# k weights of block 0 loaded ahead of two x tiles of block 1, and k of two token tiles computed between their q and the q of the next two

## The chip, the cores and the metric

The kernel runs on one core of a Trainium2 chip. A core has five engines that run at the same time, each through its own list of instructions: TensorE (PE; its weight loads are listed apart as PEld), VectorE (DVE), ScalarE (ACT), GpSimd (POOL) and SyncE (SP), which here only issues DMA transfers. The metric is the device time of one execution in microseconds (us). Before the change it is 202.04, the median of three runs (201.27 to 202.22).

## The reference

```python
xn = _layernorm(x)                       # x: 1 x 2048 x 512, bf16
# A: 32 heads of 16; W = 8 keys at distances 0, 2, .. 14
q, k, v = split(xn @ wqkv)
logits = einsum('bhsd,bhswd->bhsw', q, kg) * scale      # kg: k gathered at pos - 2*w
attn = _softmax(where(mask, logits, -1e9))
a = einsum('bhsw,bhswd->bhsd', attn, vg).reshape(B, S, D) @ wo
# B: gated MLP, F = 1376, Fh = 688
z = gelu(xn @ w_in)
z1, z2 = z[..., :Fh], _layernorm(z[..., Fh:])
g = einsum('ts,bsf->btf', w_sp, z2) + b_sp[None, :, None]   # w_sp: 2048 x 2048
return x + a + einsum('bsf,fd->bsd', z1 * g, w_out)
```

## The kernel before

**Tiling.** The 2048 tokens are 16 tiles of 128. Tile (j, tb) holds the tokens from 512·tb + 128·j on; the four tiles with the same j make a block, and the work goes block by block, j = 0 to 3. x lies in `r_x` (seen through `xall`), is normalised there in place, and is transposed into `xnT`, so that the 512 features lie along the partitions in four chunks (kc). All projections read `xnT`.

**A tile's way into `xnT`.** DVE measures a tile (`bn_stats`, L213 or L217) and aggregates (`bn_aggr`, L220). The inverse root comes from ACT (`ln_root`, L223), or for block 3 from POOL (`ln_root_pool`), an addition (L226) and a power (L227) on 128x1. DVE scales the tile (`ln_apply`, L231). The tiles of block 0 and the first two of block 1 are transposed by PE into PSUM (L238, L248) and copied to `xnT` by ACT or DVE (L242, L252, L253); the others are transposed by a DMA on SP's queue (`tr_dma`, L257).

**q and k.** The q and k weights lie in `r_w` (seen through `wqk`) in four quarters each, one per kc, 128 KB. One projection of a block, `qk_part(pq, j, m, ...)` (L321), fills half of q (m = 0, 1) or half of k (m = 2, 3) in PSUM; ACT casts it into `r_qk` (L337). For block 0, q is computed tile by tile (`q_tile`, L327) as the tiles come, and k afterwards for all four tiles at once.

**Products and logits.** For half a block of queries (a group g; there are eight) DVE multiplies q with four shifted views of k in four instructions, one per chunk c (`prod_c`, L361, 128x2048, 1.22 us each). Two additions per group (`pair_add` L370, `pair_add2` L373) fold the four chunks into one, and PE sums over the 16 dimensions of a head with a matmul against `rsel` (`logits`, L381). Then come softmax, the weighted sum of v (L445, L449 on DVE), and the output projection.

**The gated MLP.** w_in's second half gives z2 (L263 on PE, gelu on ACT at L281, squares at L287), its first half z1 (L263, L312). g is w_sp·z2 (L470), 448 matmuls, with w_sp transposed by DMA.

**PSUM** is shared by two pools: `ps_mm` has three buffers of 128x1024 f32, `ps_aux` two of 128x512 f32. An instruction that wants a new tile waits until a buffer's last reader is done.

**Order.** The program is scheduled by hand: each engine runs its instructions in the order in which the program issues them. The start (loads, layernorm, q and k of blocks 0 and 1) is written out as calls. All that follows is a string, `ORDER`, of tokens that stand for steps, a name and its numbers:

```python
z1.3   z2 matmuls of tile (1,3)      zg1.3  its gelu         zs1.3  its squares
q2.3   qk projection m=3, block 2    qc2.3  its cast         p1.2   product of group 1, chunk 2
a1 b1  the two additions of group 1  L1     its logits       Lc1    their cast
X0 Xg0 z1 matmuls and gelu           G0 U0  g matmuls, gate  w3     a DMA transpose of w_sp
```

Of the kernel before, what the change touches and what calls it, by code (L numbers as in the profile page):

```python
# [7 lines left out]
BF16 = mybir.dt.bfloat16  # L8
F32 = mybir.dt.float32
# [30 lines left out]
CHUNKS = (1, 1, 1, 1, 1, 1, 1, 1)  # L40
ORDER = """
z1.3 z2.0 z1.2 z2.2 zg1.3 p0.1 zg2.0 zg1.2 q2.2 zg2.2 p0.3 zs2.2 q2.3 p1.2 qc2.2 p1.3 q2.1 qc2.3 p1.0
z1.0 p0.2 qc2.1 w3 z2.1 p0.0 zg1.0 zs1.0 q2.0 p2.2 zg2.1 a1 z2.3 qc2.0 w2 zg2.3 p2.3 halo zs2.0 z3.0 p2.0 z1.1
w0 zg3.0 b1 z0.1 zg1.1 p2.1 zs2.3 X0 a0 zg0.1 z3.2 Xg0 zs1.1 z3.3 a2 zg3.2 z3.1 zs1.2 zg3.3 z0.2 b0 zg3.1 X4
b2 zg0.2 zs3.3 L0 L1 Xg4 q3.1 p3.2 zs3.1 p3.0 Lc0 q3.0 Lc1 p3.1 qc3.1 q3.2 p3.3 qc3.0 zs0.1 a3 z0.3 qc3.2 q3.3
zg0.3 p4.1 zs1.3 p4.0 z0.0 qc3.3 X1 p4.2 zg0.0 zs0.3 X2 p4.3 Xg1 X5 st.0 zs2.1 st.1 a4 Xg2 L2 V6 zs0.2 zs3.2
b3 Xg5 V2 b4 Vc6 zs0.0 p5.3 L3 V5 zs3.0 p5.2 Vc2 V1 st.2 p5.1 Vc5 p5.0 V0 st.3 a5 w4 Lc2 Vc1 V4 st.4 Vc0 w1
N1.1 V3 N2.0 Vc4 N1.0 b5 Lc3 V7 N0.0 Vc3 M0.0 N1.2 M0.1 L5 N0.2 L4 Vc7 N3.3 X6 N0.1 M0.2 N0.3 late X3 N3.1
N1.3 N2.1 G0.0 N2.2 Xg6 N2.3 N3.2 N3.0 G0.1 p7.1 G0.2 M0.3 G0.3 p7.2 G4 p6.0 Gi0 w6 Lc4 p6.3 Xg3 p6.2 E0 p7.3
G3 p6.1 U0 S0.0 p7.0 a6 w9 G1 Gi3 Gi4 S0.1 b6 a7 G2 Gi1 w7 U1 S0.2 b7 S0.3 w5 S0.4 Lc5 R0 L6 L7 G6 Lc6 A0 Gi2  # L50
Lc7 U2 U4 mask T4 U3 M1.0 A1 T2 G7 A2 Gi6 w8 A3 wo1.2 A4 T0 A5 X7 M1.1 Gi7 A6 wo1.3 xr0 G5 A7 Xg7 A8 w10 M1.2
A9 w12 U7 A10 X8 Gi5 A11 X10 T1 A12 G8 Xg10 A13 Xg8 wo1.0 A14 T7 M1.3 A15 G9 Gi8 A16 A17 E1 A18 A19 wo0.2
wo0.3 G10 wo0.1 U6 wo1.1 U5 Gi9 wo0.0 A20 T3 S1.0 S1.1 A21 X9 S1.2 G12 A22 S1.3 Gi10 T5 A23 S1.4 T6 A24 Xg9
w15 A25 X15 A26 Gi12 w14 X12 R1 Xg15 X11 A27 Xg12 w11 A28 O0 Xg11 A29 A30 A31 Or0 O1 A32 A33 A34 Or1 U8 Oh0.0
A35 A36 Oh0.1 Fe0.0 A37 Fe0.1 A38 G14 Fe0.2 Fe0.3 F0.2 F0.0 F0.1 s0.0 A39 s0.1 F0.3 A40 xr1 A41 Oh1.0 w13 A42
U10 Oh1.1 Fe1.0 U9 T8 Gi14 A43 Fe1.1 A44 T10 X13 A45 G11 s0.2 T9 A46 s0.3 F1.0 A47 A48 G13 F1.1 Gi11 s1.1 Xg13
U11 U12 Fe1.2 A49 T12 A50 A51 X14 A52 G15 Xg14 Fe1.3 U14 Gi13 F1.3 F1.2 A53 s1.2 T11 A54 T14 A55 O2 Gi15 s1.0
A56 U15 U13 T15 A57 Or2 xr2 Oh2.0 A58 A59 s1.3 Oh2.1 T13 Fe2.0 Fe2.1 xr3 F2.0 O3 Fe2.2 Fe2.3 F2.2 F2.1 s2.0
s2.2 F2.3 s2.1 s2.3 Or3 Of Oh3.1 end
# [10 lines left out]
def kernel(  # L70
# [98 lines left out]
    def load_wqk(E, s):  # L169
        for kc in range(C):  # L170
            E.dma_start(wqk[:, s, kc], A_wqkv[kc * P:(kc + 1) * P, s * D:(s + 1) * D])

    def load_x(E, j, b0, b1):
        for tb in range(b0, b1):
            E.dma_start(xall[:, j, tb], xblk[j][:, tb])
# [4 lines left out]
    load_x(A, 0, 2, 4)  # L180
    load_wqk(SP, 0)
    load_x(SP, 1, 0, 2)
    load_wqk(SP, 1)
    load_x(SP, 1, 2, 4)
    load_x(SP, 2, 0, 4)
    for kc in range(C):
        SP.dma_start(w_z2[:, kc], B_w_in[kc * P:(kc + 1) * P, FH:F])
# [21 lines left out]
    def ln_stats(i, parts=1):  # L209
        j, tb = i % 4, i // 4  # L210
        w = D // parts
        for h in range(parts):
            V.bn_stats(stats[:, i, 6 * h:6 * h + 6], xall[:, j, tb, w * h:w * h + w])  # L213
        ln_agg(i, parts)

    def ln_bn(i):
        V.bn_stats(stats[:, i, 0:6], xall[:, i % 4, i // 4, :])  # L217

    def ln_agg(i, parts=1):
        V.bn_aggr(mv[:, i, :], stats[:, i, 0:6 * parts])  # L220

    def ln_root(sl):
        A.activation(rstd[:, sl], mv[:, sl, 1], ACT.Abs_reciprocal_sqrt, bias=eps_t[:])  # L223

    def ln_root_pool(i):
        G.tensor_tensor(rstd[:, i:i + 1], mv[:, i, 1:2], eps_t[:], ALU.add)  # L226
        G.tensor_tensor(rstd[:, i:i + 1], rstd[:, i:i + 1], mhalf[:], ALU.pow)  # L227

    def ln_apply(i):
        j, tb = i % 4, i // 4  # L230
        V.tensor_scalar(xall[:, j, tb, :], xall[:, j, tb, :], mv[:, i, 0:1], rstd[:, i:i + 1],  # L231
                        ALU.subtract, ALU.mult)

    def tr(i):
        j, tb = i % 4, i // 4
        pt = ps_aux.tile([P, C, P], BF16, name="pt", tag="aux")
        for c in range(C):
            PE.transpose(pt[:, c, :], xall[:, j, tb, c * P:(c + 1) * P], ident[:])  # L238
        return pt

    def tr_copy(i, pt, c0=0, c1=C):
        A.copy(xnT[:, c0:c1, i * P:(i + 1) * P], pt[:, c0:c1, :])  # L242

    def tr2(i):
        j, tb = i % 4, i // 4
        pts = [ps_aux.tile([P, 2, P], BF16, name="pt", tag="aux") for _ in range(2)]
        for c in range(C):
            PE.transpose(pts[c // 2][:, c % 2, :], xall[:, j, tb, c * P:(c + 1) * P], ident[:])  # L248
        return pts

    def tr_copy2(i, pts):
        A.copy(xnT[:, 0:2, i * P:(i + 1) * P], pts[0][:])  # L252
        V.tensor_copy(xnT[:, 2:4, i * P:(i + 1) * P], pts[1][:])  # L253

    def tr_dma(i):
        j, tb = i % 4, i // 4
        SP.dma_start_transpose(xnT[:, :, i * P:(i + 1) * P], xall[:, j, tb, :])  # L257
# [66 lines left out]
    def q_tile(tb, kcs):  # L324
        for kc in kcs:
            for c in range(C):
                PE.matmul(pqs[c // 2][:, c % 2, tb * P:(tb + 1) * P], wqk[:, 0, kc, c:D:C],  # L327
                          xnT[:, kc, 4 * tb * P:(4 * tb + 1) * P], start=(kc == 0 and tb % 2 == 0), stop=(kc == C - 1 and tb % 2 == 1))
# [252 lines left out]
    def blk(j):  # L581
        return [4 * tb + j for tb in range(TB)]

    def col(i):
        return slice(i, i + 1)

    def blk_cols(j):
        return slice(j, NT, 4)

# [4 lines left out]

    t0, i1 = blk(0), blk(1)
    i2, i3 = blk(2), blk(3)
    warm_up(10)
    for n in range(2):
        ln_stats(t0[n], 2)
        ln_root(col(t0[n]))  # L600
    for n in range(2):
        ln_apply(t0[n])
    pts = [tr(t0[n]) for n in range(2)]
    tr_copy(t0[0], pts[0], 0, 2)
    tr_copy(t0[0], pts[0], 2, 4)
    tr_copy(t0[1], pts[1], 0, 2)
    warm_up(2, 1)
    pqs = [qk_tile() for _ in range(3)]
    ln_stats(t0[2])
    ln_root(col(t0[2]))  # L610
    tr_copy(t0[1], pts[1], 2, 4)
    q_tile(0, (0, 1))
    q_tile(0, (2,))
    q_tile(1, (0, 1))
    q_tile(0, (3,))
    ln_bn(t0[3])
    ln_apply(t0[2])
    ln_agg(t0[3])
    pt2 = tr2(t0[2])
    q_tile(1, (2, 3))  # L620
    ln_root(col(t0[3]))
    tr_copy2(t0[2], pt2)
    ln_apply(t0[3])
    q_tile(2, (0, 1))
    pt3 = tr2(t0[3])
    q_tile(2, (2, 3))
    tr_copy2(t0[3], pt3)
    q_tile(3, (0, 1))
    q_tile(3, (2, 3))
    ln_stats(i1[0])  # L630
    ln_root(col(i1[0]))
    qk_copy(pqs[0], 0, 0)
    ln_stats(i1[1])
    ln_root(col(i1[1]))
    qk_part(pqs[2], 0, 2, 0, 4, (0,))
    ln_apply(i1[0])
    qk_part(pqs[2], 0, 2, 0, 4, (1,), kcs=range(2))
    pt = tr(i1[0])
    qk_part(pqs[2], 0, 2, 0, 4, (1,), kcs=range(2, 4))
    ln_stats(i1[2])  # L640
    qk_copy(pqs[1], 0, 1)
    ln_root(col(i1[2]))
    ln_apply(i1[1])
    tr_copy(i1[0], pt)
    ln_bn(i1[3])
    ln_apply(i1[2])
    tr_dma(i1[2])
    ln_agg(i1[3])
    pq3 = qk_tile()
    qk_part(pq3, 0, 3, 0, 4, (0,), kcs=range(2))  # L650
    pt = tr(i1[1])
    qk_part(pq3, 0, 3, 0, 4, (0,), kcs=range(2, 4))
    tr_copy(i1[1], pt)
    ln_root(col(i1[3]))
    ln_apply(i1[3])
    tr_dma(i1[3])
    load_x(SP, 3, 0, 4)
    qk_part(pq3, 0, 3, 0, 4, (1,))
    qk_copy(pqs[2], 0, 2)
    qk_copy(pq3, 0, 3)  # L660
    for n in range(4):
        ln_stats(i2[n])
    ln_root(slice(2, 7, 4))
    ln_root(slice(10, 15, 4))
    A.preload_act_table_set("gelu_apprx_tanh_and_others")
    table[0] = "gelu"
    for i in i2:
        ln_apply(i)
        tr_dma(i)
    for n in range(3):  # L670
        ln_stats(i3[n])
        ln_root_pool(i3[n])
    ln_apply(i3[0])
    tr_dma(i3[0])
    ln_stats(i3[3])
    ln_root_pool(i3[3])
    for i in i3[1:3]:
        ln_apply(i)
        tr_dma(i)
    pqs = [qk_tile() for _ in range(3)]  # L680
    for c in range(3):
        qk_part(pqs[c], 1, c, 0, 2)
    pa3 = ps_aux.tile([P, 2, 2 * P], F32, name="pa3", tag="aux")
# [73 lines left out]
```

## Time and profile before

The profile is one execution. "Span" reaches from its first instruction to its last; the three timed runs are beside it. Busy time is the sum of an engine's instructions and overlaps among engines.

| | us |
|---|---|
| span of the profiled execution | 199.9 |
| timed runs | 202.22, 201.27, 202.04 |
| PE busy from 0 to 6.4 / 6.4 to 160 / 160 to 199.9 | 4.65 / 153.60 / 37.16 |
| DVE busy from 18 to 33 / 33 to 64 | 14.42 of 15.00 / 30.77 of 31.00 |
| ACT busy from 18 to 33 / 33 to 64 | 12.69 / 29.21 |
| POOL busy from 18 to 33 / 33 to 64 | 4.25 in 8 instructions / 15.94 in 2 |
| one product (L361) / one large addition (L370) on DVE | 1.22 / 2.29 |
| one load of a weight quarter, of an x tile, issue to landing (medians) | 3.6 / 3.0 |

The windows show that PE has no idle time between 6.4 and 160. TensorE's granted clock is 1.000 in every window. A share of busy time is an average; whether an engine sets the end is read from the chain of waits and from the idle time just ahead of its instructions.

### The profile page before, as it was taken

Reading aid. Unit: us, or ns where it says so; the run is one execution under the profiler, and the core shown is the slowest. Engines: PE = TensorE matmul, PEld = TensorE weight load, DVE = VectorE, ACT = ScalarE, POOL = GpSimd, SP = SyncE. Lnnn points to the kernel's source line nnn. Section 1 sums busy time; section 2 is a strip of 40 time slices with the busy share of each in tenths; the row PEclk is TensorE's granted clock in tenths of the full one; section 3 lists DMA queues with packets and bytes.
Section 4 is the critical chain, followed back from the end, with each engine's and each line's share of the span. In section 5 each row is a group of like instructions: output and inputs, shape, how many; then the busy total and the mean of one; then the engine's idle time right before and its main releaser. Section 6 shows DMA issues by size and latency. Waiting matters only on the chain.

```text
span 199.9 us, 4102 instructions
## 1 busy us (share of the span) xinstructions
PE 195.4 (98%) x1691; PEld 123.9 (62%) x1691; DVE 184.6 (92%) x249; ACT 103.9 (52%) x175; POOL 22.0 (11%) x23
## 2 busy tenths in 40 slices
PE   7899999999999999999999999999999999999994
PEld 2869756665566666666656666666544646664562
DVE  5789899999999999999979999999999999999624
ACT  3586978899899976453431523708402230331400
POOL 3000800699500000000000000000000000000000
DMA  5986548950000096524477999199940297219863
GB/s 160 266 244 163 106 78 240 234 113 3 0 0 3 3 157 115 167 64 100 61 152 161 239 220 192 49 217 180 192 85 0 81 208 169 72 32 127 215 209 105
DMA packets 66562, 25.91 MB, mean 130 GB/s; under 512 B 56496, under 2 KB 66288, under 8 KB 66288
## 3 DMA queue, kind: packets, MB, share of 16 engines
q1 hardware_dynamic: 65824, 25.18, 58.4%
q10 hardware_dynamic: 720, 0.48, 0.8%
q8 instruction: 13, 0.21, 0.4%
q14 instruction: 5, 0.04, 0.1%
HBM read 10.13 MB, written 2.10 MB: 61 GB/s over the span
## 4 chain that ended last, share of the span: by engine, by line
PE 95%; DMA 1%; DVE 1%; SPq 0%; ACT 0%; issue 0%
PE pg L470 37%; PE pz L263 19%; PE pq L321 11%; PE pv L431 7%; PE po L553 7%; PE po L523 6%; PE pa L553 2%; PE pq L327 2%; DMA r_x<-in_A_x_dram 1%; PE pl L381 1%; PE pa L321 1%; PE po L532 1%; PE pb L523 1%; PE pt L238 0%; DVE r_pr L541 0%; DVE stats L213 0%
## 5 line engine op out<-in xcount | busy, mean ns | idle before, releaser
L470 PE MATMUL pg<-z,r_qk 128*128 128x344 bf16 x448 | 66.8, 309 | 0.0
L470 PEld LDWEIGHTS <-r_qk 128*128 128x128 bf16 x448 | 43.8, 98 | 22.0 <-issue 0.4
L445 DVE TENSOR_TENSOR r_pr<-r_x,r_w 128x2048 bf16<-128x2048 bf16 x32 | 38.4, 1220 | 1.3 <-PE pl L381 1.0
L263 PE MATMUL pz<-w_z,xnT 128*128 128x344 bf16 x256 | 39.3, 309 | 0.0
L449 DVE TENSOR_TENSOR r_pr<-r_pr 128x2048 bf16<-128x2048 bf16 x28 | 33.9, 1219 | 0.4
L263 PEld LDWEIGHTS <-xnT 128*128 128x128 bf16 x256 | 25.0, 98 | 13.2 <-issue 0.4
L476 ACT ACTIVATE gs<-pg,b_col 128x688 bf16<-128x688 f32 x16 | 13.2, 834 | 35.4 <-PE pg L470 26.4
L361 DVE TENSOR_TENSOR r_pr<-r_qk 128x2048 bf16<-128x2048 bf16 x24 | 27.9, 1222 | 0.2 <-ACT r_qk L337 0.2
L321 PE MATMUL pq<-xnT,r_w 128*128 128x512 bf16 (+1 forms) x128 | 23.8, 339 | 0.0
L321 PEld LDWEIGHTS <-r_w 128*128 128x128 bf16 x144 | 15.9, 114 | 7.6 <-issue 0.4
L536 ACT CAST r_qk<-po 128x512 bf16<-128x512 f32 x10 | 5.5, 588 | 22.7 <-PE po L553 22.7
L699 POOL CAST b_col<-b 128x16 f32<-128x16 bf16 x1 | 15.7, 15704 | 11.8 <-DMA b<-in_B_b_sp_dram 11.8
L337 ACT CAST r_qk<-pq 128x1024 bf16<-128x1024 f32 x15 | 14.9, 1015 | 2.4 <-PE pq L321 2.3
L312 ACT ACTIVATE r_uz<-pz 128x688 bf16<-128x688 f32 x16 | 11.7, 740 | 6.6 <-PE pz L263 6.5
L523 PE MATMUL po<-r_lg,r_pr 32*128 32x512 bf16 x192 | 14.5, 375 | 0.0
L431 PE MATMUL pv<-xnT,r_w 128*32 128x512 bf16 x256 | 14.2, 379 | 0.0
L553 PEld LDWEIGHTS <-r_uz 128*128 128x128 bf16 x85 | 8.0, 98 | 9.5 <-issue 1.1
L370 DVE TENSOR_TENSOR r_pr<-r_pr 128x4096 bf16<-128x4096 bf16 x6 | 13.7, 2289 | 0.0
L553 PE MATMUL po<-r_w,r_uz 128*128 128x512 bf16 x60 | 13.6, 380 | 0.0
L281 ACT ACTIVATE z<-pz 128x688 bf16<-128x688 f32 x16 | 11.9, 744 | 1.5 <-PE pz L263 1.5
L287 ACT ACTIVATE junk<-z 128x688 bf16<-128x688 bf16 x16 | 12.4, 774 | 0.1
L431 PEld LDWEIGHTS <-r_w 128*32 128x32 bf16 x256 | 9.5, 138 | 4.3
(88 smaller groups left out, 200.3 us busy)
## 6 DMA issues: line engine op xcount, KB each, us to landing
r_lg<-in_A_wo_dram SPq DMA_DIRECT2D x8, 256.0 KB, 4.2
r_x<-in_A_x_dram SPq DMA_DIRECT2D x12, 128.0 KB, 3.0
out_dram<-r_qk SPq DMA_DIRECT2D x12, 128.0 KB, 2.1
r_w<-in_A_wqkv_dram SPq DMA_DIRECT2D x8, 128.0 KB, 3.6
r_qk<-in_A_x_dram SPq DMA_DIRECT2D x8, 128.0 KB, 2.2
w_z<-in_B_w_in_dram SPq DMA_DIRECT2D x4, 172.0 KB, 4.4
w_z<-in_B_w_in_dram SPq DMA_DIRECT2D x1, 688.0 KB, 5.5
r_w<-in_B_w_out_dram SPq DMA_DIRECT2D x1, 640.0 KB, 6.5
```

The costliest lines, as they stand in the source:

```text
L263: PE.matmul(pz[:, hh, 0:FHALF], xnT[:, kc, i * P:(i + 1) * P], wz[:, kc, hh * FHALF:(hh + 1) * FHALF], start=(kc == 0), stop=(kc == C - 1))
L321: PE.matmul(pq[:, cc, p0 * P:(p0 + b1 - b0) * P], wqk[:, sd, kc, c0 + cc:D:C], xv[:, kc, b0:b1, j, :], start=(kc == 0), stop=(kc == C - 1))
L337: cast = A.copy(dst, pq[:, :, p0 * P:(p0 + b1 - b0) * P].rearrange("p c (b t) -> p c b t", b=b1 - b0))
L361: prod = V.tensor_tensor(pr[g % 3][:, c].rearrange("p w b t -> p b w t"), q3.unsqueeze(2).broadcast_to([P, TB, 4, P]), k4, ALU.mult)
L370: V.tensor_tensor(pr[g % 3][:, 0:2], pr[g % 3][:, 0:2], pr[g % 3][:, 2:4], ALU.add)
L431: PE.matmul(pv[32 * tb:32 * tb + 32, dd, :], wv[:, kc, 2 * d2 + dd, :], xnT[:, kc, tb * TBS:(tb + 1) * TBS], start=(kc == 0), stop=(kc == ...
L445: V.tensor_tensor(pw_t[n], vp[:, :, off:off + P], a_sb[:, slot_w(w), ts].unsqueeze(1).broadcast_to([P, DH, P]), ALU.mult)
L449: V.tensor_tensor(pw_t[n] if dst is None else dst, pw_t[n], pw_t[m], ALU.add)
L470: PE.matmul(pg[:, hh, 0:FHALF], wsp[n][:, k, :], z2[:, k, hh * FHALF:(hh + 1) * FHALF], start=(k == 0), stop=(k == NT - 1))
L523: PE.matmul(pc, op[32 * tb:32 * tb + 32, d, o * P:(o + 1) * P], wo_r[32 * tb:32 * tb + 32, d, cs], start=(d == 8), stop=False, tile_positi ...
L553: mm = PE.matmul(pc, uT[:, o % 2, m, tb * P:(tb + 1) * P], wout[:, m, cs], start=False, stop=(m == MCH - 3))
L699: G.tensor_copy(b_col[:], b16[:])
```

## The change

The start becomes a second token string, `START`, which takes the place of the written-out calls and of the first lines of `ORDER`; from `L0 L1` on `ORDER` is the same. The same projections, products and additions are made. New are:

- SP loads all eight quarters of the q and k weights ahead of the first two x tiles of block 1; before, the quarters of k stood behind them. The loads of block 3's x stand later, in the order (3,3), (3,0), (3,2) and then (3,1).
- Of tiles (0,0) and (0,1), the half that comes by ACT's queue is measured first.
- Tile (0,0) is transposed into two tiles of `ps_aux`, two chunks each, with two warm-up matmuls between; tile (0,1) into a tile of `ps_mm`.
- q of tiles (0,0) and (0,1) goes as before in steps of one tile (`qt`); m = 2 of k of these two follows in steps of two tiles and one kc (`kp0.0` and `kp0.1` among the q and transpose steps, `kp0.2`, `kp0.3` after them); q of the other two goes in steps of two tiles (`qw`).
- The projections of block 1 have another order (`y`, half a block each). Statistics of block 2 stand together ahead of their aggregations.
- On DVE, products of groups 0 and 1 (`p1.1 p0.3 p0.1 p1.2`, then `p0.2 p1.3`) stand between the statistics, aggregations and scalings of block 3.

Counted over the program, PE has 1683 matmuls instead of 1691: 32 of 128 columns and 8 of 512 fewer, 32 of 256 more. DVE has 249 instructions in both.

The string is one line in the file and is broken here:

```diff
+START = """
+warm10.4 ls0.0.1 ls0.0.0 la0.0 lr0.0 ls0.1.1 ls0.1.0 la0.1 lr0.1 ln0.0 lt0.0.0.2 lc0.0.0.2 warm2.1
+lt0.0.2.4 ln0.1 lt0.1.0.4.1 lc0.0.2.4 lc0.1.0.2 lc0.1.2.4 ls0.2 la0.2 ls0.3 lr0.2 la0.3 lr0.3 ln0.2
+qt0.0 qt0.1 qt0.2 qt1.0 qt1.1 kp0.0 qt1.2 qt0.3 lt0.2.0.2 lc0.2.0.2 kp0.1 ln0.3 lt0.3.0.2 lc0.3.0.2.1
+qt1.3 lt0.3.2.4 lc0.3.2.4.1 lt0.2.2.4 lc0.2.2.4 qw0 qw1 qw2 qw3 ls1.0 la1.0 lr1.0 c0 ls1.1 ln1.0 la1.1
+lr1.1 kp0.2 kp0.3 kp1.0 kp1.1 kp1.2 kp1.3 km3.0.0.2 lt1.0 ls1.2 ln1.1 lt1.1 la1.2 ls1.3 la1.3 c1 lr1.2
+lc1.0.0.4 lc1.1.0.4 ln1.2 lr1.3 ld1.2 c2 ls2.3 ln1.3 ld1.3 ls2.2 km3.0.2.4 km3.1.0.4 c3 y0.0 y3.0 lx3.3.4
+lx3.0.1 lx3.2.3 la2.3 ls2.1 ls2.0 la2.2 lr2.2.2 la2.1 la2.0 lr2.0.2 gelu ln2.0 ln2.3 ld2.3 ln2.2 ld2.2
+ln2.1 y1.0 y2.0 y2.1 yc2 y0.1 yc0 y1.1 yc3.0 yc1 ls3.0 ls3.2 p1.1 z1.2 y3.1 yc3.1 z1.3 z2.2 zg1.2 zg2.2
+zg1.3 ls3.3 p0.3 la3.2 p0.1 la3.0 p1.2 ld2.1 ld2.0 q2.3 lx3.1.2 lp3.2 lp3.0 qc2.3 zs2.2 z1.0 zg1.0 zs1.0
+q2.2 qc2.2 z2.0 zg2.0 q2.1 qc2.1 ls3.1 la3.1 lp3.1 ln3.0 ld3.0 z2.1 zg2.1 z2.3 p0.2 la3.3 p1.3 lp3.3
+ln3.2 ln3.1 ln3.3 p1.0 ld3.2 ld3.3 ld3.1 lv halo lz lb w3 p0.0 a1 q2.0 zg2.3 zs2.0 qc2.0 zs2.3 z1.1 z3.0
+zg1.1 zg3.0 p2.2 w2 p2.3 p2.0 w0 b1 a0 z3.3 z3.2 z0.1 zg3.3 zg3.2 zs3.3 b0 p2.1 a2 b2 zg0.1 z3.1 X0 z0.2
+zg3.1 X4 zs1.1 zg0.2 zs1.2 Xg0
+"""
...
-    load_wqk(SP, 0)
-    load_x(SP, 1, 0, 2)
-    load_wqk(SP, 1)
-    load_x(SP, 1, 2, 4)
-    load_x(SP, 2, 0, 4)
...
+    load_wqk(SP, 0, 0, 1)
...
+    load_wqk(SP, 1, 3, 4)
+    load_x(SP, 1, 0, 1)
...
+    load_x(SP, 2, 3, 4)
...
+    def qk_step(sd, ms, tb, kc):
+        for m in ms:
+            for cc in range(2):
+                PE.matmul(p0[m][:, cc, tb * P:(tb + 1) * P], wqk[:, sd, kc, 2 * (m % 2) + cc:D:C],
+                          xnT[:, kc, 4 * tb * P:(4 * tb + 1) * P], start=(kc == 0 and tb % 2 == 0),
+                          stop=(kc == C - 1 and tb % 2 == 1))
...
+    def q_pair(kc):
+        for m in range(2):
+            for cc in range(2):
+                PE.matmul(p0[m][:, cc, 2 * P:4 * P], wqk[:, 0, kc, 2 * m + cc:D:C],
+                          xnT[:].rearrange("p k (b j t) -> p k b j t", b=TB, j=4)[:, kc, 2:4, 0, :],
+                          start=(kc == 0), stop=(kc == C - 1))
+
+    def k_pair(h, kc):
+        for cc in range(2):
+            PE.matmul(p0[2][:, cc, 2 * h * P:(2 * h + 2) * P], wqk[:, 1, kc, cc:D:C],
+                      xnT[:].rearrange("p k (b j t) -> p k b j t", b=TB, j=4)[:, kc, 2 * h:2 * h + 2, 0, :],
+                      start=(kc == 0), stop=(kc == C - 1))
...
+    steps = {"warm": warm_up, "ls": ln_stats, "la": ln_agg, "lr": ln_root, "lp": ln_root_pool, "ln": ln_apply, "lt": tr,
+             "lc": tr_copy, "ld": tr_dma, "qt": q_step, "kt": k_step, "kk": k3_step, "km": k_wide, "qw": q_pair, "kp": k_pair, "nb": ln_shift, "c": c0_copy, "y": y_part, "yt": y_tile, "yc": y_copy,
+             "lx": lambda j, b0, b1: load_x(SP, j, b0, b1), "lw": load_z2, "lv": load_v, "lz": load_z1, "lb": load_b,
...
-    for tok in ORDER.split():
+    for tok in START.split() + ORDER.split():
```

In `lt0.0.2.4` the numbers are j, tb and the first and last chunk, a fifth number asks for a tile of `ps_mm`; in `lc` a fifth number puts the copy on DVE; `kp0.1` is tiles 0 and 1 with kc = 1; `y3.1` is m = 3, second half of block 1; `lv`, `lz` and `lb` load the v weights, the weights of z1 and the bias b_sp.

## The prediction

> **What bounds the kernel now.** I read the page's busy rows first, then the chain of waits in order of time, then the timeline of DVE and POOL.
>
> ```profile
> PE 195.4 (98%) x1691; PEld 123.9 (62%) x1691; DVE 184.6 (92%) x249; ACT 103.9 (52%) x175; POOL 22.0 (11%) x23
> PE   7899999999999999999999999999999999999994
> DVE  5789899999999999999979999999999999999624
> PE 95%; DMA 1%; DVE 1%; SPq 0%; ACT 0%; issue 0%
> ```
>
> PE is busy in every slice but the first and the last, and holds 95% of the chain; DVE is nearly as full behind it. From the first q matmul to the last output matmul the chain never leaves PE. So a change at the start gains only by starting PE earlier, and loses whenever PE must wait. The head of the chain in order of time (start, duration, what):
>
> ```profile
> 4.20 0.76 DVE stats L213 x2
> ...
> 5.23 0.30 ACT rstd L223
> ...
> 5.56 0.42 DVE r_x L231
> 5.98 0.05 issue
> 6.03 0.40 PE pt L238 x4
> 6.42 0.11 PE pwm L592 x2
> 6.53 1.35 PE pq L327 x24
> ```
>
> The reader is to see that the second x tile's statistics, root and scaling set PE's start, and that two warm-up matmuls (0.11) stand on the chain.
>
> The second place to look is where DVE is nearest to holding PE up. The logit matmuls of product group 3 (token L3) read what b3 adds:
>
> ```profile
> 61.78 2.35 DVE L373 TENSOR_TENSOR r_pr<-r_pr 128x2048 bf16<-128x2048 bf16 x2
> 64.20 0.39 PE L381 MATMUL pl<-r_pr,rsel 128*32 128x512 bf16 x4
> ```
>
> The first of the two additions, 1.22 long, is b3: done at 63.00. L3 starts at 64.20, and the shortest delay of the trace from DVE's end to PE's start is 0.05. DVE may come 1.15 later there before PE waits. L0 has less (b0 ends at 46.56, L0 starts at 47.11), but in the new order b0 stands ahead of p2.1, a2 and b2 and comes earlier, not later.
>
> Third, POOL beside DVE's products:
>
> ```profile
> 21.89 0.55 POOL L227 TENSOR_TENSOR rstd<-rstd,mhalf 128x1 f32<-128x1 f32 x1
> 23.01 1.74 POOL L227 TENSOR_TENSOR rstd<-rstd,mhalf 128x1 f32<-128x1 f32 x1
> 23.12 1.22 DVE L361 TENSOR_TENSOR r_pr<-r_qk 128x2048 bf16<-128x2048 bf16 x1
> 24.79 0.41 DVE L231 TENSOR_SCALAR r_x<-r_x,mv,rstd 128x512 bf16<-128x512 bf16 x1 [0.44 <-POOL rstd L227]
> 36.59 15.70 POOL L699 CAST b_col<-b 128x16 f32<-128x16 bf16 x1 [11.84 <-DMA b<-in_B_b_sp_dram]
> ```
>
> The same power operation takes 0.55 beside statistics and 1.74 when a product starts 0.11 after it; a cast of 16 columns takes 15.70 while DVE runs products and additions back to back, and ends at 52.29, right after the first gap between two of them (52.24 to 52.27). A POOL operation hardly advances while a DVE product runs.
>
> **The change, part by part.** I walk the changed order of each engine with these rows' durations; every us below is the walk's.
>
> *Head.* The two halves of tile (0,1) land at 3.99 (ACT queue) and 4.17 (SP queue). Before, the SP half is measured first: 4.20, then 4.54. Now the ACT half starts at 4.02 and the second at 4.36: 0.18 earlier. The two warm-ups move into the gap before the second tile's transposes, at most 0.11 more. The first copy to xnT starts after two transposes, not four; the first q matmul needs its end, so not all of it counts: 6.38 becomes 6.18. Gain 0.20 (bounds 0.18 and 0.29).
>
> *Matmuls.* 32 fewer of 128 columns (0.056 apart), 32 more of 256 (0.109), 8 fewer of 512 (0.216): -1.79+3.50-1.73, nothing. Waits for copies of tiles 2 and 3 were 0.07+0.07; now the two halves each need an aux buffer back: 0.07+0.14. PE's net lead after block 0: 0.2.
>
> *Loads.* All are 128 KB on SP's queue, so the order decides the landing. The k weights' first quarter takes the place of x tile (1,0), landed at 7.18; its matmul comes at 7.29. I take 0; if it needs the 3.54 of the weight loads instead of the 3.17 of that x load, it lands at 7.55: 0.25 lost. Tile (1,0) now lands at 9.76, and DVE, there by 9.2, waits 0.5. Before, DVE had waits of 0.40 and 0.57 for transposes there; the totals come out equal within 0.1. The transposes by DMA for block 1 reach PE with 0.2 in hand, those of block 2 for the k matmul q2.3 also with 0.2 (landing rows 2.4 to 3.6 after issue).
>
> *DVE, blocks 1 and 2.* Statistics now follow one another and the aggregations come after them. An aggregation right behind its own statistics starts 0.70 after them, another instruction 0.58, so each pair pulled apart saves 0.12. DVE is through block 2 at 18.53 instead of 18.95, 0.4 early.
>
> *DVE, block 3 and the first products, where it turns.* Before, the sixteen tiles are finished before the products run freely (from 25.11), and DVE idles 0.9 in this stretch. Now p1.1, p0.3, p0.1 and p1.2 stand between the statistics of block 3. Its waits: 0.6 and 0.3 for tiles (3,0) and (3,2), whose loads stand behind two DMA transposes (1.30 each on SP) and are issued at 16.4 to 17.5; 0.2 and 0.8 for copies of block 1's q and k (p0.3 needs k's last pair, and y3.1 now stands behind z1.2); 0.1 more of the 0.12s; and the roots on POOL. lp3.2 starts at 24.7 under p0.1, and cannot get its 0.19 done before 27.0, since the gap between p0.1 and p1.2 is one aggregation, 0.10. Its power operation and lp3.0 then run to 28.4: ln3.0 waits 0.7. lp3.1's power operation stands under p0.2 and p1.3 until 31.5 (ln3.1 waits 0.1), then lp3.3 costs ln3.3 0.5. Together 3.4 instead of 0.9: DVE is 2.0 late at 33.
>
> *What absorbs it.* At 57.0 DVE of before waits for ACT's copy of q3.1's k (0.5 in the walk, 0.16 shown as idle); now it is late and doesn't wait. Back-to-back pair additions add 0.3. At b3 DVE is 1.9 late: done at 64.9.
>
> *The sum.* PE reaches L3 at 64.0 and waits until 64.95: 0.9. Less the 0.2 lead: **+0.7**. Behind L3 the order is unchanged, the smallest slack left is 0.3 to 0.5, and PE carries the delay to the end. The profiled execution is 199.9; the median 202.04 lies 2.1 above its span, taken as unchanged. 200.6 of span, **202.8**. SP's later loads shift too: v and the first gate's weights go out at 36.8 and 37.5 instead of 30.2 and 30.8; with 5.46 to landing they are there at 42.9, X0 comes at 43.5. Covered by 0.5.
>
> **Rivals.**
> 1. *POOL is no obstacle*: the roots take 0.74 beside products. For: three of four power operations took 0.55. Against: the two rows of 1.74 and 15.70. DVE keeps 1.3 of its waits, its lateness at b3 falls below 1.15, PE doesn't wait, and the lead of 0.2 stays: 201.8. It decides as long as DVE loses less than 1.35. Chance 0.2.
> 2. *Landings are late as well*: the weight quarter (0.25) and a block 2 transpose with the 3.57 that one took. These shift both engines, so they add: +1.2, 203.2. For: slack of 0.1 to 0.2 each; against: the same bytes in the same places. Chance 0.17.
> 3. *The product waits instead*: POOL holds and DVE stands. lp3.1's power operation starts at 28.7, just ahead of p0.2: p0.2 waits 0.5, ln3.1 no longer 0.1; +1.1, 203.1. The trace has one such meeting: POOL at 23.01, product at 23.12 on time. Chance 0.08.
>
> The Trainium skill ("SBUF — State Buffer", "Who interferes with whom") says that a DVE instruction with two SBUF inputs and a POOL instruction that reads SBUF exclude one another, and that the one that started first keeps the port for its whole length. Exclusion agrees with the 1.74; who goes first does not, since POOL had started first there and was the one delayed. By that rule the time would be rival 3's.
>
> **How the numbers follow.** The forecast has 0.55. No change is within 0.5%, about 1.0 us, what a measurement here can tell from none (the runs before span 0.95). The forecast's own range is 202.2 to 203.4, with the spread of medians more than 1.0 above in a third of it; rival 2 exceeds it in three quarters, rival 3 in over half, rival 1 falls below in a quarter: 0.18+0.13+0.05 gives slower 0.36, rival 1's quarter (0.05) and 0.03 of the forecast (a stall of PE that the walk sees and the chip does not) faster 0.08, the rest 0.56. The range takes rival 1's centre less 0.3 at one end and rival 2's plus 0.5 at the other: 201.5 to 203.7.
>
> **What would show it.** Right: the chain's first q matmul near 6.35 instead of 6.53; a PE wait of about 0.9 before the logits of group 3, released by DVE's pair addition; POOL additions or powers of over 2 us near 25 and 29; DVE idle of about 3 between 18 and 33. Wrong: PE without a wait at L3 (rival 1), waits of PE at 7.3 or 25 for a DMA (rival 2), products that start late beside short POOL operations (rival 3), or a wait in the g matmuls, which nothing here foresees.

## The result and the profile after

Over 11 runs each the changed kernel takes 202.21 us in the median and the kernel before 201.68 (the three runs shown earlier are among the latter). The ratio is 1.0029, with a 95% interval of 1.0020 to 1.0039: slower by 0.4 to 0.8 us, inside what the prediction called no change and on the side it forecast. The profiled execution spans 200.4 us against 199.9.

The busy row and the shares of the chain, from the page of the changed kernel:

```profile
PE 196.3 (98%) x1683; PEld 125.8 (63%) x1683; DVE 184.6 (92%) x249; ACT 103.7 (52%) x175; POOL 9.8 (5%) x23
PE 74%; DVE 18%; DMA 3%; POOL 2%; issue 1%; SPq 0%; ACT 0%; POOLq 0%
```

DVE is busy for 184.6 us, as before. What is new is that DVE is on the chain: 18% of it instead of 1%, and POOL has 2%. The chain no longer stays on PE from the first q matmul to the end. Its rows in order of time (start, duration, what) show where it leaves PE and comes back:

```profile
3.65 3.85 DMA r_w<-in_A_wqkv_dram
7.55 0.41 PE pq L359 x2
...
22.01 0.89 PE pa L325 x8
22.92 0.59 ACT r_qk L404
23.54 1.23 DVE r_pr L428
24.94 1.08 POOL rstd L228
26.09 1.48 POOL rstd L229
...
63.42 1.15 DVE r_pr L440
64.61 0.40 PE pl L448 x4
```

It runs from the load of the first k quarter (landed at 7.50) to kp0.0 at 7.55, over PE to y3.1 (22.01), its cast, product p0.3, the roots on POOL, and then down DVE to b3 (63.42) and the third group of logits. Behind that it is PE again.

DVE's waits between 18 and 33 stand in its timeline; the brackets hold the idle time ahead of a row and what ended it:

```profile
19.49 1.29 DVE L213 BATCH_NORM_STATS2 stats<-r_x 128x6 f32<-128x512 bf16 x2 [0.65 <-DMA r_x<-in_A_x_dram]
21.15 1.22 DVE L428 TENSOR_TENSOR r_pr<-r_qk 128x2048 bf16<-128x2048 bf16 x1 [0.37 <-ACT r_qk L404]
...
23.54 1.23 DVE L428 TENSOR_TENSOR r_pr<-r_qk 128x2048 bf16<-128x2048 bf16 x1 [0.56 <-ACT r_qk L404]
...
28.39 0.41 DVE L241 TENSOR_SCALAR r_x<-r_x,mv,rstd 128x512 bf16<-128x512 bf16 x1 [0.41 <-POOL rstd L229]
```

The four waits are 1.99. A fifth, of 0.12, stands inside a row and has no bracket: ln3.3, the last scaling of block 3, starts at 31.91, behind its root on POOL, which ends at 31.87. In this stretch of 15.00 DVE is busy for 12.86, so it idles 2.14; before it was busy for 14.42 and idled 0.58. Further on DVE is 1.82 late (the products of group 3 start at 49.43 against 47.61), and 0.26 of that is gone at b3, in part because DVE of before waits 0.16 for a cast at 57.0 and this one doesn't. So it is 1.56 late at b3, which equals the difference of the idle times by chance:

```profile
63.34 2.36 DVE L440 TENSOR_TENSOR r_pr<-r_pr 128x2048 bf16<-128x2048 bf16 x2
64.61 0.40 PE L448 MATMUL pl<-r_pr,rsel 128*32 128x512 bf16 x4
```

b3 is the first of the two additions, 1.22 long: done at 64.56, against 63.00 before. The logits follow 0.05 later, at 64.61 against 64.20. So 1.56 of lateness met 1.15 of slack, and 0.41 was left. From there to PE's last matmul the distance is the same: PE ends 0.42 later (197.58 against 197.16).

How much of this is a stall of PE can be read from two starts. From the first group of logits (L0) to group 3 (L3) PE takes 17.09 when nothing holds it, as before (47.11 to 64.20). Here it takes 17.39 (47.22 to 64.61): a stall of 0.30. L0 itself is 0.11 late, and the two make up the 0.41. Below, "L0 to L3" is this distance, and 17.09 means no stall.

### The profile page after: what moved, and what is told of

Same layout as the page of the kernel before. It is cut to its first block, busy times and chain, and to the rows that moved or that the text cites. A ratio compares the mean times of both kernels' runs of the same rounds, so it can differ in the third digit from the quotient of the medians.

```text
span 200.4 us, 4093 instructions
## 1 busy us (share of the span) xinstructions
PE 196.3 (98%) x1683; PEld 125.8 (63%) x1683; DVE 184.6 (92%) x249; ACT 103.7 (52%) x175; POOL 9.8 (5%) x23
## 4 chain that ended last, share of the span: by engine, by line
PE 74%; DVE 18%; DMA 3%; POOL 2%; issue 1%; SPq 0%; ACT 0%; POOLq 0%
PE pg L537 37%; PE pz L267 7%; DVE r_pr L428 7%; PE po L620 7%; PE po L590 6%; PE pv L498 5%; DVE r_pr L437 4%; PE pq L325 3%; DVE r_uz L428 2%; PE pa L620 2%; DMA r_w<-in_A_wqkv_dram 2%; DVE r_pr L440 2%; POOL rstd L229 1%; POOL rstd L228 1%; DVE r_uz L437 1%; DMA r_x<-in_A_x_dram 1%
## 5 line engine op out<-in xcount | busy, mean ns | idle before, releaser
L267 PE MATMUL pz<-w_z,xnT 128*128 128x344 bf16 x256 | 39.8, 309 | 0.0
L325 PE MATMUL pq<-xnT,r_w 128*128 128x512 bf16 (+1 forms) x120 | 22.3, 337 | 0.0
L325 PEld LDWEIGHTS <-r_w 128*128 128x128 bf16 x136 | 15.0, 114 | 6.8 <-issue 0.4
L498 PEld LDWEIGHTS <-r_w 128*32 128x32 bf16 x256 | 10.1, 138 | 3.5
L590 PEld LDWEIGHTS <-r_pr 32*128 32x128 bf16 x272 | 7.5, 93 | 6.6 <-issue 1.0
```

Of the source, the lines that this page charges most:

```text
L267: PE.matmul(pz[:, hh, 0:FHALF], xnT[:, kc, i * P:(i + 1) * P], wz[:, kc, hh * FHALF:(hh + 1) * FHALF], start=(kc == 0), stop=(kc == C - 1))
L325: PE.matmul(pq[:, cc, p0 * P:(p0 + b1 - b0) * P], wqk[:, sd, kc, c0 + cc:D:C], xv[:, kc, b0:b1, j, :], start=(kc == 0), stop=(kc == C - 1))
L498: PE.matmul(pv[32 * tb:32 * tb + 32, dd, :], wv[:, kc, 2 * d2 + dd, :], xnT[:, kc, tb * TBS:(tb + 1) * TBS], start=(kc == 0), stop=(kc == ...
L590: PE.matmul(pc, op[32 * tb:32 * tb + 32, d, o * P:(o + 1) * P], wo_r[32 * tb:32 * tb + 32, d, cs], start=(d == 8), stop=False, tile_positi ...
```

## Experiments

Ratios are to the kernel before, timed beside each variant on the same chip (5 to 12 runs of a variant, 23 or 25 of the kernel before), with 95% intervals. Starts of matmuls come from each variant's trace, which is one execution.

**k_later.** All k steps of block 0 behind all q steps, loads as changed.

```diff
-... qt1.1 kp0.0 qt1.2 ... lc0.2.0.2 kp0.1 ln0.3 ... lr1.1 kp0.2 kp0.3 ...
+... qt1.1 qt1.2 ... lc0.2.0.2 ln0.3 ... lr1.1 kp0.0 kp0.1 kp0.2 kp0.3 ...
```

> The changed kernel with its four k steps of the first two tile pairs (kp0.0 and kp0.1) moved behind all q steps of block 0, loads as changed. Theory 1 (the wait of PE for the first k quarter, up to 7.55, delays q and k of block 1 and through their casts DVE as well): L0 starts near 46.9 instead of 47.22, the third group of logits near 64.25 instead of 64.61, the run is 0.35 us shorter than the changed kernel, ratio to before near 1.001. Theory 2 (only DVE's own lateness between 18 and 33 sets the end, and PE's early wait lies in slack): L0 earlier, but the third group still near 64.6, ratio near 1.003.

Ratio 1.0029 (1.0016 to 1.0043); L0 at 47.30, L0 to L3 17.38. PE's wait near 7.5 is gone, and yet L0 is not earlier. PE's timeline shows what took its place:

```profile
7.73 0.29 PE L252 MATMUL pt<-ident,r_x 128*128 128x128 bf16 x2
8.21 0.28 PE L252 MATMUL pt<-ident,r_x 128*128 128x128 bf16 x2 [0.19 <-DVE r_x L241]
```

The q steps run out before the last tile of block 0 is scaled, and PE loses 0.36 between these two rows, more than the 0.26 that the move was to save. In the changed kernel the k steps fill just this gap. Neither theory named this wait. The ratio is theory 2's, but neither theory is tested: PE's early delay was exchanged for another one, not removed, and L0 didn't come earlier.

**y31_first.** The last quarter of block 1's projections ahead of the z matmuls.

```diff
-... p1.1 z1.2 y3.1 yc3.1 z1.3 ...
+... p1.1 y3.1 yc3.1 z1.2 z1.3 ...
```

> The changed kernel with y3.1 and its copy ahead of z1.2, so that the last pair of block 1's k is cast 1.2 us earlier. Theory 1 (DVE's lateness at b3 is the sum of its waits, and 0.56 of it stands before p0.3): DVE's idle before p0.3 falls from 0.56 to under 0.2, third group of logits near 64.2, ratio near 1.001. Theory 2 (the next wait, POOL's roots, takes the place): idle before ln3.0 grows by as much, third group still at 64.6, ratio near 1.003.

Ratio 1.0008 (0.9999 to 1.0018). DVE's two products follow without a wait (their rows have no bracket), although this execution's x tiles came later still:

```profile
19.88 1.42 DVE L213 BATCH_NORM_STATS2 stats<-r_x 128x6 f32<-128x512 bf16 x2 [1.07 <-DMA r_x<-in_A_x_dram]
21.43 1.22 DVE L428 TENSOR_TENSOR r_pr<-r_qk 128x2048 bf16<-128x2048 bf16 x1
22.57 0.69 DVE L213 BATCH_NORM_STATS2 stats<-r_x 128x6 f32<-128x512 bf16 x1
23.32 1.22 DVE L428 TENSOR_TENSOR r_pr<-r_qk 128x2048 bf16<-128x2048 bf16 x1
```

b3 starts at 63.12 (63.34 in the changed kernel) and L0 to L3 is 17.09: no stall. The wait before ln3.0 is 0.41 as ever. So theory 1's saving is there in the ratio. The third group itself is at 64.58, not 64.2, because in this execution PE was late already at L0 (47.49), with 0.28 of it at 18.3, for the transposes by DMA of block 1.

**roots_early.** Aggregations and roots of block 3 ahead of the products.

```diff
-... ls3.0 ls3.2 p1.1 ... ls3.3 p0.3 la3.2 p0.1 la3.0 p1.2 ... lp3.2 lp3.0 ... la3.3 p1.3 lp3.3 ln3.2 ...
+... ls3.0 la3.0 lp3.0 ls3.2 la3.2 lp3.2 p1.1 ... ls3.3 la3.3 lp3.3 p0.3 p0.1 p1.2 ... p1.3 ln3.2 ...
```

> The changed kernel with the aggregation and root of each tile of block 3 right behind its statistics, ahead of the products. Theory 1 (POOL's roots, held up under products, cost DVE some 0.4 to 0.5): POOL's additions take 0.2 and its powers 0.6, DVE does not wait before ln3.0, third group of logits near 64.2, ratio near 1.001. Theory 2 (the wait is taken over by the copies of block 1's q and k): DVE's idle before p1.1 and p0.3 grows by 0.4, nothing gained, ratio near 1.003.

Ratio 1.0022 (1.0013 to 1.0032); L0 to L3 17.09. DVE no longer waits for a root before ln3.0, and the stall at L3 is gone. POOL's operations still met products (an addition of 1.08, powers of 1.62 and 1.42, not the 0.2 and 0.6 of theory 1), but far enough ahead of the scalings. The ratio gives back about a quarter of the loss only, and its interval overlaps that of the changed kernel. In the profiled execution PE is late at L0 already (47.73), 0.29 of it at 18.5 for a transpose by DMA and 0.18 from a later first q matmul; whether these hold for the other runs isn't shown. Here and in y31_first the first of these transposes took 1.81 on SP, against 1.31 in the changed kernel; why is open.

**x3_early.** Two x tiles of block 3 loaded ahead of the transposes by DMA of block 1.

```diff
-... ln1.2 lr1.3 ld1.2 ... y3.0 lx3.3.4 lx3.0.1 lx3.2.3 la2.3 ...
+... ln1.2 lr1.3 lx3.0.1 lx3.2.3 ld1.2 ... y3.0 lx3.3.4 la2.3 ...
```

> The changed kernel with the loads of x tiles (3,0) and (3,2) ahead of the two transposes by DMA of block 1. Theory 1 (the wait of 0.65 for x is hidden anyway, since p1.1 behind it waits for the copy of block 1's q): the idle before the statistics goes, that before p1.1 grows from 0.37 to about 1.0, third group stays near 64.6, ratio near 1.003. Theory 2 (the waits add up): DVE 0.65 earlier at b3, third group near 64.2, ratio near 1.001. If the transposes that now stand behind the loads come late, PE waits for them near 16 and the time rises.

Ratio 1.0048 (1.0034 to 1.0062); L0 to L3 17.39. DVE has its tiles at once, and pays at the next wait; PE pays for the transposes:

```profile
18.52 1.72 PE L325 MATMUL pq<-xnT,r_w 128*128 128x256 bf16 x14 [0.39 <-DMA xnT<-r_x]
```

```profile
18.66 1.28 DVE L213 BATCH_NORM_STATS2 stats<-r_x 128x6 f32<-128x512 bf16 x2
21.64 1.23 DVE L428 TENSOR_TENSOR r_pr<-r_qk 128x2048 bf16<-128x2048 bf16 x1 [1.70 <-ACT r_qk L404]
```

p1.1's wait grew from 0.37 to 1.70 (PE's lateness at 18.5 is part of it). The waits for x and for the copies don't add up: the later one decides. The mishap that the expectation named came true at 18.5 instead of 16.

**stats_together.** Three tiles of block 3 measured, rooted and scaled around the first product.

```diff
-... ls3.0 ls3.2 p1.1 ... ls3.3 p0.3 la3.2 p0.1 la3.0 p1.2 ... lp3.2 lp3.0 ... lp3.1 ln3.0 ... p0.2 la3.3 p1.3 lp3.3 ln3.2 ln3.1 ln3.3 ...
+... ls3.0 la3.0 lp3.0 ls3.2 la3.2 lp3.2 ls3.3 la3.3 lp3.3 p1.1 ln3.0 ln3.2 ln3.3 ... p0.3 p0.1 p1.2 ... lp3.1 ... p0.2 ln3.1 p1.3 ...
```

> The changed kernel with tiles (3,0), (3,2) and (3,3) of block 3 measured, aggregated, rooted and scaled on DVE around the first product, ahead of the products p0.3, p0.1 and p1.2; PE's and SP's orders as changed. Theory 1 (the order of DVE in block 3 makes it stand for copies and for POOL; PE then waits for b3): DVE's idle time between 18 and 33 falls from 2.14 to about 1.0 (the wait for x stays), PE no longer waits at the third group of logits (about 0.3 earlier), ratio near 1.001. Theory 2 (what costs is the order on PE, y3.1 behind z1.2): ratio stays near 1.003.

Ratio 1.0056 (1.0041 to 1.0071): worse. L0 to L3 is 17.09, and the waits for copies are gone from DVE, as theory 1 said. DVE still idles 1.72 between 18 and 33, not 1.0, since the root of the last tile on POOL now costs it 0.71. The time went at a place that neither theory had:

```profile
26.30 1.89 PE L325 MATMUL pq<-xnT,r_w 128*128 128x512 bf16 x8 [0.84 <-DMA xnT<-r_x]
```

q2.3 needs the last transpose of block 2. It was issued at 22.52 and landed at 26.06, 3.54 later; in the changed kernel it was issued at 22.10 and landed at 24.62, 2.52 later. What differs is SP's queue behind it: with block 3 scaled early, its first transpose goes out at 24.51 instead of 28.83. In the kernel before it took as long (issued 22.29, the next at 23.61, landed at 25.86, 3.57 later), with q2.3 placed later. But a transpose close behind can't be the whole cause: in the same traces others that were followed by the next after 1.3 landed in 2.4 to 2.6 (in stats_together the one issued at 18.64 landed at 21.18). The cause stays open.

**together_kp.** The same, with kp0.0 two q steps later.

```diff
-... qt1.1 kp0.0 qt1.2 qt0.3 lt0.2.0.2 ...
+... qt1.1 qt1.2 qt0.3 kp0.0 lt0.2.0.2 ...
```

> stats_together and, besides, kp0.0 two q steps later (0.45 us of q matmuls), so that the first k quarter has landed. Theory 1 (PE stands 0.26 for that quarter and has no other wait in its place, unlike with all k steps behind q): L0 another 0.2 to 0.3 earlier than in stats_together, ratio near 0.9995. Theory 2 (waits for the tiles 2 and 3 of block 0 take its place again): as stats_together.

Ratio 1.0053 (1.0039 to 1.0068). PE doesn't wait for the k quarter, and nothing takes its place up to the first z matmul: from the first q matmul to that one 14.31, against 14.49 in stats_together. But stats_together's execution had no such wait either, as its first q matmul came only at 6.43 and kp0.0 at 7.78; so the two traces don't show what the move saves. The expected ratio was lost with stats_together's wait, which is here too (1.03 at 26.0); by the ratios alone the two can't be told apart.

**head_on_before.** On the kernel before: the ACT half first, the two PSUM tiles, the warm-ups between.

```diff
-        for h in range(parts):
+        for h in reversed(range(parts)):
...
-    pts = [tr(t0[n]) for n in range(2)]
-    tr_copy(t0[0], pts[0], 0, 2)
-    tr_copy(t0[0], pts[0], 2, 4)
+    pt0 = [ps_aux.tile([P, 2, P], BF16, name="pt", tag="aux") for _ in range(2)]
+    for c in range(C):
+        PE.transpose(pt0[c // 2][:, c % 2, :], xall[:, 0, 0, c * P:(c + 1) * P], ident[:])
+        if c == 1:
+            A.copy(xnT[:, 0:2, 0:P], pt0[0][:])
+            warm_up(2, 1)
...
```

> The kernel before with three parts of the change alone: the half by ACT's queue measured first, tile (0,0) transposed into two PSUM tiles and (0,1) into one of the large ones, the two small warm-ups between. Theory 1 (PE is full from its first q matmul on): first q matmul 0.2 earlier, near 6.18, and the whole run 0.2 shorter, ratio near 0.999. Theory 2 (what is gained ahead of the first q matmul is lost at the next wait, the transposes of tiles 2 and 3): ratio 1.000.

Ratio 0.9994 (0.9984 to 1.0005). The first q matmul starts at 6.03 instead of 6.38, and PE then stands for the third weight quarter of q:

```profile
6.03 0.61 PE L327 MATMUL pq<-xnT,r_w 128*128 128x128 bf16 x8
7.08 1.08 PE L327 MATMUL pq<-xnT,r_w 128*128 128x128 bf16 x16 [0.44 <-DMA r_w<-in_A_wqkv_dram]
```

What was gained is lost again, as theory 2 has it, but at another wait than it named: in this execution the landing of the weights sets the pace of the start. L0 is at 47.39, 0.28 later than before.

**x_first.** k_later with the loads of before.

```diff
+    load_x(SP, 1, 0, 1)
+    load_x(SP, 1, 1, 2)
     load_wqk(SP, 1, 0, 1)
...
     load_wqk(SP, 1, 3, 4)
-    load_x(SP, 1, 0, 1)
-    load_x(SP, 1, 1, 2)
```

> k_later with the loads in the order of before (x tiles (1,0) and (1,1) between the weights of q and k). Theory 1 (the order of these loads is not felt: DVE reaches tile (1,0) only at 9.1, and its wait there was for copies): as k_later, ratio near 1.003. Theory 2 (an earlier x tile lets DVE run ahead in block 1): DVE's lateness at b3 falls, ratio under 1.002.

Ratio 1.0025 (1.0016 to 1.0034), L0 to L3 17.38: as k_later. The order of the loads that gives the change its name is not where the time went. (As in k_later, PE waits for the last tile of block 0 instead of the k quarter.)

**y31_roots_kp.** The three repairs together, without stats_together's early scaling.

```diff
-... qt1.1 kp0.0 qt1.2 qt0.3 lt0.2.0.2 ... ls3.0 ls3.2 p1.1 z1.2 y3.1 yc3.1 z1.3 ... ls3.3 p0.3 la3.2 p0.1 la3.0 p1.2 ...
+... qt1.1 qt1.2 qt0.3 kp0.0 lt0.2.0.2 ... ls3.0 la3.0 lp3.0 ls3.2 la3.2 lp3.2 p1.1 y3.1 yc3.1 z1.2 z1.3 ... ls3.3 la3.3 lp3.3 p0.3 p0.1 p1.2 ...
```

> The changed kernel with three repairs: y3.1 and its copy ahead of z1.2, aggregations and roots of block 3 ahead of the products, kp0.0 two q steps later. Theory 1 (the loss is DVE's lateness at b3 plus PE's wait for the first k quarter, and nothing else): third group of logits 17.09 after the first (no stall), no wait of PE near 7.5, ratio near 0.9998, the changed kernel's loss gone. Theory 2 (each repair opens another wait, as when block 3 was scaled early): ratio over 1.001.

Ratio 1.0004 (0.9996 to 1.0013): the loss is gone. L0 to L3 is 17.09, no wait near 7.5. The first q matmul starts at 5.81, 0.57 earlier than before, but L0 (47.08) only 0.03 earlier. 0.42 of it is lost again at one place:

```profile
17.89 1.28 PE L325 MATMUL pq<-xnT,r_w 128*128 128x256 bf16 x10 [0.26 <-DMA xnT<-r_x]
```

y2.1 waits for the second transpose by DMA of block 1, which landed at 17.84.

**head_q.** head_on_before, with q of the second tile ahead of the third weight quarter.

```diff
-    q_tile(0, (2,))
     q_tile(1, (0, 1))
+    q_tile(0, (2,))
```

> The head of the change alone on the kernel before, with q of tile (0,1) for the first two weight quarters ahead of q of tile (0,0) for the third, so that PE does not stand 0.61 for that quarter. Theory 1 (PE is full from its first q matmul on, so what starts earlier ends earlier): first q matmul near 6.0 to 6.2, the wait near 7.1 falls to 0.2 or less, ratio near 0.998. Theory 2 (the start is bound by the weights' landing and by the tiles 2 and 3, not by the first transposes): ratio near 0.9995 again.

Ratio 0.9992 (0.9971 to 1.0012). The wait near 7.1 is gone, but in this execution the first q matmul came at 6.28 and L0 at 47.08, 0.02 earlier than before. The interval holds both theories, and the medians are the same (201.62 and 201.63); no version was found that is faster than the kernel before beyond doubt.

## Why the prediction was right, step by step

The forecast was +0.7, by a stall of 0.9 at L3 less a lead of 0.2; it came out at +0.41 in the trace and +0.53 in the medians. The place, the engine and the stretch that makes DVE late were right. That the number came so near is in part luck: the stall came out 0.6 smaller than forecast, and PE's lead of 0.2 became a delay of 0.11, and these two misses offset each other by half. Of the signs that the prediction named, the stall at L3 behind DVE's addition came, at a third of its size, and DVE's idle time was 2.14 instead of about 3; POOL operations of over 2 us didn't come (the longest took 1.48); and a sign of rival 2 came, PE's wait for a load at 7.5. The absolute 202.8 is another 0.4 too high because it rests on the median of three runs, 202.04; over 11 runs it is 201.68. The sizes of the terms:

- *Head.* First q matmul at 6.17, forecast 6.18. This too is luck: DVE had scaled the second tile at 5.44 instead of 5.97, 0.53 earlier and not 0.18, while slow warm-up matmuls held PE until 5.29 (last section). In the kernels with this head the first q matmul came anywhere from 5.81 to 6.43.
- *The first k quarter.* Forecast as in time, with 0.25 lost if it landed at 7.55; its last part landed at 7.50, the chain has kp0.0 at 7.55, and PE lost 0.26. With 0.07 more at the buffers of the last transposes, as forecast, the lead of 0.21 became a delay of 0.11 at L0. This half of rival 2 came true, and as rival 2 has it the loss adds to the end: the k quarter is on the chain, and what PE loses ahead of y3.1 goes through to L3 (below). No run takes this wait alone away; k_later and x_first put another in its place. The other half did not come: the last transpose of block 2 landed at 24.62, ahead of q2.3 at 25.05.
- *DVE ahead of block 3.* Forecast 0.4 early, measured 0.22 (the scalings of block 2 end at 18.84 against 19.06): block 2's roots on ACT made DVE wait 0.42 at 17.5, which the working left out.
- *Waits for x tiles and copies.* Forecast 0.9 and 1.0; measured 0.65 and 0.93. They don't add up as the working has it: all but the last, for y3.1's cast ahead of p0.3, are swallowed by that one (below).
- *POOL's roots.* Forecast 1.3 in three places; measured 0.41 at ln3.0 and 0.12 at ln3.3. This is the term that was mis-sized most. It held that an addition could not finish in the gap of an aggregation (0.10) between two products. It did:

```profile
24.94 1.07 POOL L228 TENSOR_TENSOR rstd<-mv,eps_t 128x1 f32<-128x1 f32 x1 [22.24 <-DVE mv L220]
26.09 1.48 POOL L229 TENSOR_TENSOR rstd<-rstd,mhalf 128x1 f32<-128x1 f32 x1
...
28.60 0.62 POOL L229 TENSOR_TENSOR rstd<-rstd,mhalf 128x1 f32<-128x1 f32 x1
30.11 1.08 POOL L228 TENSOR_TENSOR rstd<-mv,eps_t 128x1 f32<-128x1 f32 x1 [0.90 <-DVE mv L220]
```

The addition of 24.94 ends at 26.01, 0.05 after product p0.1 (24.77, 1.19 long); the power behind it at 27.57, 0.4 after p1.2 (25.98, 1.19). And the power of 28.60, beside p0.2 from 28.72, took 0.62, where 2.8 had been forecast.
- *The sum at L3.* DVE late by 1.56 instead of 1.9, PE late by 0.11 instead of early by 0.2: a stall of 0.30 instead of 0.9. (The waits that the prediction lists add up to 3.3, not 3.4, and its steps behind 33 lead from 2.0 to 1.8, not 1.9; this hardly matters.) The sum lets DVE's lateness and PE's lead run side by side. The runs show that b3 follows PE, since DVE waits for y3.1's cast on the way. Three variants that leave this part of the order as it is have y3.1 and L3 on their chains so (k_later, x_first, x3_early):

```profile
22.09 0.89 PE pa L325 x8
64.69 0.40 PE pl L448 x4
...
21.86 0.89 PE pa L325 x8
64.46 0.40 PE pl L448 x4
...
22.50 0.89 PE pa L325 x8
65.10 0.40 PE pl L448 x3
```

L3 starts 42.60 behind y3.1 each time, as in the changed kernel (22.01 to 64.61), although DVE's wait for the x tiles of block 3 was 0.57, 0.18 and none there, and 0.65 in the changed kernel. So the end is the sum of what PE loses ahead of y3.1 (0.11 at L0) and of the stall behind it (0.30). By these figures the k quarter's 0.26 stands in the end in full, and without it the loss would be some 0.15; this is an estimate, no run shows it.
- *Behind L3.* Nothing changed, as forecast.

Of the rivals, POOL as no obstacle was half right (0.53 of the 1.3 was left), rival 2 was right about the weight quarter, and no product waited for POOL. y31_first, roots_early and y31_roots_kp bear out that DVE's path from y3.1's cast over POOL's roots made the stall: the first takes the wait for the cast away, the second those for the roots, the third all of them, and each has L0 to L3 back at 17.09. In the ratios this is clear for y31_first and y31_roots_kp; for roots_early it is shown by one trace alone.

The Trainium skill ("SBUF — State Buffer", "Who interferes with whom") says that a DVE instruction with two SBUF inputs contends with a POOL instruction that reads SBUF, that the port pair they share is an exclusive lock, and that issue order decides who blocks; that the first one has it for the whole instruction stands there in the sentence on DVE's two-port modes. Where the product was first the traces agree (1.07 and 1.08 instead of 0.19, ending 0.05 after the product). Where POOL was first they don't settle it: with leads of 0.11 and 0.12 a power took 1.74 before and 0.62 here, and neither product waited.

## What to carry to other kernels

When one engine is full, look for the place where the next one has least slack, and follow the chain back from there to the last wait that the full engine ends. The waits behind that one count, less the slack; those ahead of it are swallowed; and what the full engine loses ahead of it goes through to the end. A token moved into a gap is often covering a wait; of four single repairs here two only moved the wait (k_later to the next transposes, x3_early to a copy and a transpose). And moving an instruction on one engine moves what it releases: stats_together freed DVE and sent transposes of block 3 out earlier; in the same stretch one of block 2 landed 1.0 later, and PE lost more there than it won. Whether the first caused the second isn't shown.

## What the runs showed of the hardware

**TensorE's rate at the start.** The ten large warm-up matmuls are the same in both kernels; the timelines of the kernel before and of the changed one:

```profile
1.04 3.88 PE L592 MATMUL pwm<-warm 128*128 128x512 bf16 x10 [1.04 <-DVE warm L190]
```

```profile
1.04 4.45 PE L650 MATMUL pwm<-warm 128*128 128x512 bf16 x10 [1.04 <-DVE warm L188]
5.29 0.42 PE L252 MATMUL pt<-ident,r_x 128*128 128x128 bf16 x2
```

A matmul of 512 columns starts every 0.427 at first and every 0.217 later, one of 128 every 0.107 and later 0.056. The step came at about 4.2 in the kernel before, at 5.9 here, and in twelve traces anywhere from about 3.8 to 6.9; the granted clock of the profile reads 1.00 there all the same, in both kernels. In the changed kernel the slow warm-ups held PE until 5.29, though the first tile was scaled at about 5.0. The first q matmul scatters from 5.81 (step at 3.9) to 6.43 (step at 6.7) in the kernels with the new head, by three times the 0.20 that the edit was to gain. The Trainium skill ("TensorE: Matmul & The Clock Gate", "Part 1: The HAM clock gate (the "warmup" mystery)") describes this step, from half rate to full after a busy window of some 3.4 us that runs freely, and puts it at around 4 us into the matmuls, give or take 0.5. The pitches agree; the time doesn't, as the step came 2.7 to 5.9 after the first matmul (1.04).

**A cast on POOL.** The cast of b took 15.70 us before, 1.96 in the changed kernel and 0.24 in stats_together. It ends at DVE's next gap: in all twelve traces DVE's row has exactly one gap from the cast's start to its end, and the cast ends 0.05 to 0.06 behind the start of that gap (in the changed kernel DVE's gap is from 43.53 to 43.57 and the cast ends at 43.59).
